# Softmax sums laid over 32 partitions of 48 numbers instead of 128 of 12, in a clustered attention and FFT-filter kernel

## The chip, the cores and the metric

One core of a Trainium2 chip runs the kernel. The metric is the device time of one execution in microseconds; the times of several executions are given by their median. The profile is of one execution. Its engines are PE (TensorE, matrix products), PEld (TensorE's weight loads), DVE (VectorE), ACT (ScalarE), POOL (GpSimd) and SP (SyncE, which here only issues transfers).

## The reference

Inputs are q, k, v of 4 batches x 8 heads x 768 tokens x 64 numbers, and 16 centroids for each head. Everything is float32.

```python
q_assign = np.argmax(np.einsum('bhsd,hcd->bhsc', q_n, c_n), axis=-1)     # q, k, c with unit norm
k_assign = np.argmax(np.einsum('bhsd,hcd->bhsc', k_n, c_n), axis=-1)
mask = q_assign[:, :, :, None] == k_assign[:, :, None, :]
scores = np.where(mask, scale * q @ k.T, -1e9)
attn = np.exp(scores - scores.max(-1)); attn = attn / (attn.sum(-1) + 1e-9)
x = (attn @ v)                                   # heads side by side: 4 x 768 x 512
x1, x2, x3 = split(x @ w_proj, 3)
y = x1 * irfft(rfft(x2) * rfft(filter)) * x3     # along the 768 tokens
out = y @ w_out
```

So each token attends to the tokens of its own cluster, and the result goes through a gated filter over the whole sequence (called the hyena in the code).

## The kernel before

The work is cut into eight groups n (a batch and half of its heads), each of two pairs pr of heads, and four hyenas, one for each batch, which follow when both groups of a batch are through.

For one pair, `attention` runs over six blocks sk of 128 keys. For each block TensorE makes the scores in three pieces of 512 columns (`sc`); the operands `aug` hold q or k in 64 rows and the cluster's one-hot rows (the mask) beside them, so that the mask comes out of the same product. ScalarE turns each piece into exponentials in `p` (`exp`, L647 and L650). TensorE multiplies them with v (`pv`, L661) into a pair of PSUM banks, and VectorE adds the blocks' exponentials up into `acc` (L682; the first two blocks are added in three pieces, L678, on VectorE or GpSimd).

`acc` then holds, for each of the 1536 queries of the pair, 128 partial sums, one on each partition. They are reduced in one of two ways. The first two groups and the last one (called `late` in the code) use a product with ones (`den`, L695). The ten other pairs use transfers: three GpSimd transfers add the upper half of the partitions onto the lower half (128 to 16 rows, L715); SP writes the 16 rows to DRAM (`dd`, L719) and reads them back spread over the partitions (`dp`, L721); VectorE sums the 16 rows (L725), adds a small constant (L726) and takes the reciprocal (L728). For every pair but the last, SP writes the reciprocals to DRAM (`dr`, L729) and reads them back to all partitions (`rb`, L732), and VectorE multiplies the attention's result with them into `xT` (L761), the hyena's input. The last pair's reciprocals are spread by products on TensorE.

The `routing` of group n + 1 runs beside the attention of group n: transposes of q and k (L551), products with the centroids (L583), comparisons on VectorE (L588 to L608) and transfers of the mask rows into `aug` (L482). The hyena multiplies xT with w_proj (L798), takes the spectrum, multiplies it with the filter's (L822, L826), transforms back, folds (L887, L897), gates (L862, L900) and multiplies with w_out.

Each step is recorded by `op` with the engines that may run it and a planned cost. The order of all 1936 steps, the engine of each and the PSUM banks are read from the string `ORDER`, written by a planner beforehand: `V694` is step 694 on VectorE, `P1421:0` step 1421 on TensorE in bank 0; A is ScalarE, G is GpSimd, S is SP. Each engine runs its steps in that order and waits at each for what the step needs. A step on GpSimd with `lock=True` also waits for the last VectorE step so marked, since both use one port.

At the start TensorE makes 16 warm-up products on the tile `y` (`hot`). The filter's values are loaded into the memory of `y` and `y2` (`tables`).

Of the kernel before, what the change touches and what calls it, by code (L numbers as in the profile page):

```python
# [27 lines left out]
EPS = 1e-30  # L28
# [101 lines left out]
P149:2 A99 P249:5 S128 G132 P251:4 A151 V93 V91 A250 V90 P243:7 A252 V92 S125 P183:6 V109 P245:5 A244 G98 V107 A184  # L130
S129 P185:0 P187:7 V150 G253 A186 P190:3 S288 V110 P192:6 P194:2 A188 V147 P200:0 V111 S287 A195 P202:7 V112 A246
P204:2 V199 A191 P189:45 V113 A193 V197 A201 A203 V198 P208:3 P210:6 A205 P212:0 V114 P216:7 P196 A211 V207 A209 A213
P218:2 P220:6 A254 P224:3 V148 P226:0 G154 V115 P206 A217 A219 V119 A118 P228:1 V153 P263:7 A116 V155 P214 V117 A221
V215 A248 P293:2 P222 A227 A294 V157 A229 P255:6 V223 A225 P257:0 P295:2 A264 P297:1 P300:3 A258 P261:7 A256 P302:0
V158 P230 A298 V160 A301 A262 V231 A296 P304:6 P310:1 S352 P312:3 A305 P267:72 S291 A303 V156 A232 S292 V159 A311
P233:6 S285 V269 A259 G162 P314:0 V268 S290 P318:1 A313 P299:45 V270 A315 G161 S289 A266 V234 P320:2 S286 P322:7 A319
V271 G152 P163:3 A323 S242 P171:0 A260 P164:6 S235 V272 P326:1 V273 G307 P328:7 A165 P306 A327 V166 A167 G358 P330:1
V274 A169 P316 G353 A331 V275 G309 A329 P334:3 P172:1 A321 V168 S278 P336:7 A175 G356 P177:2 V276 S280 V170 P324 A335
G308 S277 A173 V176 S279 V174 P419:361 S236 G247 A337 A181 V317 G357 A265 P338:0 P178:7 S453 A339 P332 S454 A421 V420
A422 V325 P359:0 A179 P361:1 P363:3 P340 A362 A360 V182 G426 A364 P366:6 V237 P368:1 A342 V180 P370:0 S238 G355 P376:3  # L140
P378:7 A371 V333 P365:45 S282 G354 A369 S455 A367 P380:2 A379 S283 P384:0 V374 P386:1 A381 P388:6 S281 P392:7 V341
A377 P372 S284 A387 S239 A385 P394:2 A389 S240 V375 P396:3 P343:1 A397 V373 A395 P427:063 V383 A393 A344 S345 P400:2
P402:7 A429 P404:1 V391 P382 A430 A428 A401 P461:0 A405 V399 P463:3 P465:6 A403 P390 A466 S346 A425 V407 P468:2
P435:17 S456 A464 V241 P470:6 P472:3 P398 A471 V437 A462 G476 V436 A473 P478:6 V438 P480:0 P482:1 P486:7 A481 P488:3
V347 P406 V439 A469 S348 A433 S458 V440 A483 P409:0 S418 V441 G475 A408 S459 P490:2 A489 P494:1 P467:45 V442 S460 A495
A487 S349 V443 G477 A410 P474 A479 A491 S446 V444 P496:3 S411 V485 P498:1 P502:7 A497 P701:062 S448 A434 S445 A424
V431 S447 P484 A499 V493 S350 S452 P504:3 P506:1 S457 P492 A505 V423 A704 S412 V501 A503 S520 P500 A507 S449 A703 S451
P639:3 V509 P508 A640 S738 A702 P641:7 V413 P643:1 A510 G708 P511:3 S414 A642 G432 P646:0 A644 V512 P648:2 P650:6 A647
G706 P656:7 S513 P658:1 A649 P660:3 P645:45 S450 V351 A657 A661 V653 A651 S416 P664:0 P666:2 A659 P668:7 V655 S415
P672:3 P674:6 A669 P676:1 V707 P652 A673 S514 V654 A677 A665 V663 P709:731 A675 A667 P680:0 V671 P682:6 S741 P684:2  # L150
A681 P662 A685 A711 V515 A683 V679 P743:0 S516 P670 A710 S740 A744 A712 S735 P745:2 V417 P747:6 P750:0 P752:1 P717:37
V687 A753 A746 S518 A748 S517 P754:1 A714 V718 P760:2 G689 P678 S736 V719 A755 G758 V720 S700 A751 P686 V721 P762:6
P764:3 A688 V722 P768:7 P770:1 P772:0 A761 V723 G757 P749:45 A765 A769 V724 P776:2 A771 P778:3 P780:7 P756 A779 V759
A763 V519 A705 G690 P766 V725 A781 V726 P521:1 S728 V767 S804 P523:3 A522 S729 A777 P531:6 S727 V525 A773 S732 V524
P526:7 A532 S730 V775 G691 P784:1 S739 P786:2 P528:0 A787 S742 A527 P533:3 A713 S734 V529 P788:6 P564:2 S733 V534 A789
S737 P774 V535 A785 G537 A715 V530 S692 A565 P805:7 V536 P807:6 P809:1 P812:3 A808 V539 P814:0 P816:2 A810 P782 V783
A806 A815 P822:6 A817 P824:1 P826:7 V538 A823 P830:0 P790 A813 V791 A831 A827 P540:2 S866 A792 P543:6 G819 V542 S693
P867:307 A825 V541 S731 V544 G821 P811:45 A869 V545 A870 V546 G793 A868 P548:1 V547 A873 P832:2 P834:6 V549 G716
P551:0 A833 P838:3 V550 P818 A835 G820 V552 A839 V553 P840:7 P842:2 V829 P875:163 A843 P556:0 V554 A877 S906 P828 A841
V837 A876 G794 A878 P846:2 P566:7 A847 V557 G555 P848:1 P850:3 V694 P909:6 P559:2 A910 P836 V695 V560 A851 S696 A871  # L160
V558 S903 G562 P911:6 V567 P568:3 S907 A912 V561 P913:0 P883:76 A569 G795 V845 S908 A879 S904 A849 P570:2 A914 S698
V884 G563 V885 P916:3 P918:1 P579:0 V886 A919 P920:6 P926:7 A580 P928:1 V887 A917 P844 A921 V853 A929 S796 P572:03
A927 P852 A573 V888 G855 V574 P930:6 G872 V575 P934:1 P581:7 A931 V889 A854 G576 S797 P936:0 P583:3 V582 A882 S901
P938:6 V890 P915:45 A584 A937 V891 G923 A939 P942:7 P922 A880 V571 S896 V577 A943 S894 V925 A874 P587:30 S697 V892
P585:6 V578 G856 S895 A588 A935 P932 S893 V586 G924 A881 S902 V589 V590 P944:2 S899 P946:7 V798 P950:1 P952:6 A947
S905 P594:0 V933 P596:3 A595 A951 P940 A953 V799 V941 S800 G857 A945 P954:7 S970 P1089:0 P598:1 A955 S898 A1090 V699
P1091:6 P1093:2 P1096:7 P1098:0 P948 V949 A1099 A1092 S801 A1097 P1100:0 S802 P1106:6 A1094 P956 V957 S858 A1107 A1101
P1108:7 P600:2 A958 V592 G959 P1110:6 V591 A1109 P1114:0 P1095:45 A599 G593 A1111 V601 V597 S859 P1116:7 P1118:1
P1151:623 A1117 G1105 A1115 A1119 P609:7 A1152 V1154 S1186 P602:01 A1153 V1103 S1187 P1159:236 V1104 A603 S897 A1158
V605 G1155 S900 V604 P1102 A1161 V1113 G960 S1191 A1162 S1190 A1160 P1122:0 P1124:1 A1123 P1167:23 S1192 V803 A610  # L170
G607 P1126:6 V1168 P1112 A1127 G606 V860 A1125 V1169 A1156 P1130:0 G961 P1132:7 V861 V1170 P1134:6 S862 A1131 P1193:1
P1195:2 P1197:3 P1120 A1196 V1121 A1135 A1198 P1200:0 A1133 P1202:2 V1171 P1204:6 P1210:3 A1194 P1212:7 P1128 A1203
S864 V1172 A1201 S1188 V1129 A1211 P611:1 S962 A1163 P1214:2 S863 P1218:0 A1166 P1220:3 V612 P1136 S1185 V1173 A1213
A1205 V1137 P1222:1 A1215 P613:7 A1138 P617:62 S963 A1221 P1199:45 V608 A618 S1189 A614 V1174 P1226:3 P1228:7 P1206
A1227 V620 G1208 A1223 V1175 A1219 P1230:3 V619 A1229 P1216 G1139 S1178 V1176 A1231 G622 S1177 A1157 V964 P1234:1
S1183 P615:0 A1164 V965 G621 P1224 S966 V616 S1180 V1207 S1179 P1236:2 V1209 P1232 A1237 V865 A1235 A1165 P1238:6 V623
P1325:730 S967 A1239 V1217 S968 G1140 P1317:216 S1150 A1328 S1182 A1326 V1225 A1327 S1254 P1240 A1320 S1184 A1319
S1181 A1318 P1255:0 V1233 P1257:3 P1259:7 A1256 P626:1 A1260 A1258 P624:2 P1262:6 V969 G1141 P631:0 A625 A627 V1241
P1264:7 P629:3 A1265 A1263 P981:2 V630 G1243 P971:1 V1321 P973:7 G1324 A972 S1142 A982 P983:6 G1323 V975 A1242 S628
V974 P976:3 A632 V984 P978:1 A977 V985 P1266:2 P1272:7 V979 P1014:0 A1267 S1143 V980 P1274:3 P1276:6 S1352 V987  # L180
P1280:2 A1275 P1261:45 G1244 A1273 V986 S1358 A1281 V988 A1015 S1356 P1282:1 P1284:3 V989 P990:7 A1283 S1351 P1288:2
G1269 P993:0 V991 A1289 P1016:1 S1355 V992 A1285 P1018:2 V994 A1277 G1270 S1316 P1020:7 V1017 A1019 V995 P998:3 G996
# [46 lines left out]
def build(T):  # L229
# [386 lines left out]
    def attention(n, pr, sins):  # L616
# [88 lines left out]
        if not last:  # L705
# [5 lines left out]
            else:  # L711
# [12 lines left out]
                def gather(e):  # L724
                    T.nc.vector.tensor_reduce(T.dn, T.dp[:].rearrange("p r b -> p b r"), axis=AX, op=Alu.add)  # L725
                    T.nc.vector.tensor_scalar(T.dn, T.dn, EPS * S, None, op0=Alu.add)  # L726
# [467 lines left out]
```

## Time and profile before

| what | value |
|---|---|
| median of 3 runs | 366.29 us (366.25 to 366.62) |
| the profiled execution | 366.52 us |
| its span on the core | 364.7 us |
| PE busy | 353.9 us (97%) |
| DVE busy | 339.3 us (93%) |
| ACT busy | 271.1 us (74%) |
| POOL busy | 137.1 us (38%) |
| granted TensorE clock, mean | 0.996 |

Busy is the time in which the engine ran at least one instruction; the span goes from the first instruction to the last, and the difference to the execution's own time lies around it. "L661" is line 661 of the kernel before. A row of a group gives the line, the engine, the operation, the tiles written and read, their shapes, the count, and behind the bar the busy time in us and the mean of one in ns, then the time that the engine idled before them and what ended it. In a timeline row the start and the length come first, and idle time before it stands in brackets with what ended it.

### The profile page before, as it was taken

Reading aid. Unit: us, or ns where it says so; the run is one execution under the profiler, and the core shown is the slowest. Engines: PE = TensorE matmul, PEld = TensorE weight load, DVE = VectorE, ACT = ScalarE, POOL = GpSimd, SP = SyncE. Lnnn points to the kernel's source line nnn. Section 1 sums busy time; section 2 is a strip of 40 time slices with the busy share of each in tenths; the row PEclk is TensorE's granted clock in tenths of the full one; section 3 lists DMA queues with packets and bytes.
Section 4 is the critical chain, followed back from the end, with each engine's and each line's share of the span. In section 5 each row is a group of like instructions: output and inputs, shape, how many; then the busy total and the mean of one; then the engine's idle time right before and its main releaser. Section 6 shows DMA issues by size and latency. Waiting matters only on the chain.

```text
span 364.7 us, 8483 instructions
## 1 busy us (share of the span) xinstructions
PE 353.9 (97%) x3254; PEld 198.8 (55%) x3254; DVE 339.3 (93%) x470; ACT 271.1 (74%) x502; POOL 137.1 (38%) x167
## 2 busy tenths in 40 slices
PE   8799999999999999999999999999999999999994
PEld 4445445454555555665565555555655556475771
DVE  8899889998999999989987999999999999999992
ACT  5999989789878777898987667789969826532232
POOL 8930841122131644344143463432340363045500
PEclk9999999999999999999999999999999999999998
DMA  9990999165576568678667948375755640410214
GB/s 171 226 248 14 218 180 179 26 166 132 120 134 147 102 108 129 130 148 151 131 125 193 174 111 155 43 156 56 178 80 155 89 61 17 162 43 2 117 59 173
DMA packets 88004, 45.69 MB, mean 125 GB/s; under 512 B 76488, under 2 KB 82012, under 8 KB 87964
## 3 DMA queue, kind: packets, MB, share of 16 engines
q1 hardware_dynamic: 84076, 35.16, 40.9%
q0 software_dynamic: 2960, 9.77, 18.6%
q8 instruction: 25, 0.41, 0.5%
q10 hardware_dynamic: 928, 0.23, 0.3%
q14 instruction: 15, 0.12, 0.1%
HBM read 31.59 MB, written 7.40 MB: 107 GB/s over the span
## 4 chain that ended last, share of the span: by engine, by line
PE 77%; DVE 9%; ACT 8%; DMA 3%; issue 2%; SPq 0%; DVEq 0%
PE bank L69 33%; PE pair L661 26%; PE bank L798 6%; PE bank L551 4%; ACT p L650 3%; DVE acc L682 3%; PE bank L583 2%; DMA dn<-dd 2%; PE bank L1015 2%; ACT aug L246 2%; ACT p L647 2%; PE bank L67 2%; DMA aug<-ohT 1%; PE bank L695 1%; PE bank L470 1%
## 5 line engine op out<-in xcount | busy, mean ns | idle before, releaser
L661 PE MATMUL pair<-p,vraw 128*64 128x385 f32 x768 | 140.4, 488 | 0.0
L650 ACT ACTIVATE p<-bank 128x512 f32<-128x512 f32 x192 | 108.5, 614 | 18.0 <-PE bank L69 15.6
L682 DVE TENSOR_TENSOR acc<-p,acc 128x1536 f32<-128x1536 f32 x64 | 112.1, 1751 | 2.1
L661 PEld LDWEIGHTS pair<-p,vraw 128*64 128x64 f32 x768 | 54.5, 136 | 47.6 <-issue 38.8
L69 PE MATMUL bank<-aug,aug 80*64 80x256 bf16 (+3 forms) x708 | 78.9, 327 | 1.3 <-DMA aug<-ohT 0.7
L647 ACT ACTIVATE p<-bank 128x512 f32<-128x512 f32 x96 | 57.8, 613 | 16.8 <-PE bank L69 11.3
L69 PEld LDWEIGHTS <-aug 80*64 80x64 bf16 (+1 forms) x708 | 40.9, 109 | 42.4 <-issue 29.7
L715 POOL DMA_DIRECT2D acc<-acc x30 | 24.1, 805 | 75.1 <-DMA acc<-acc 30.6
L678 POOL TENSOR_TENSOR acc<-p,p 128x512 f32<-128x512 f32 x23 | 29.8, 1298 | 48.6 <-ACT p L650 13.6
L69 PE MATMUL bank<-xT,wpj 128*64 128x384 bf16 x480 | 46.3, 326 | 0.0
L69 PEld LDWEIGHTS <-wpj 128*64 128x64 bf16 x480 | 27.6, 110 | 15.8 <-issue 5.3
L246 ACT CAST aug<-qkP 64x768 bf16<-64x768 f32 x43 | 35.4, 829 | 0.7
L246 ACT COPY qkP<-bank 128x512 f32<-128x512 f32 (+1 forms) x56 | 28.4, 562 | 7.9 <-PE bank L69 5.8
L69 PEld LDWEIGHTS <-y 128*64 128x64 bf16 x480 | 23.8, 110 | 11.5 <-issue 2.4
L822 DVE TENSOR_TENSOR tm<-bank,hm 128x512 f32<-128x512 f32 x44 | 27.9, 682 | 0.9 <-POOL y L826 0.2
L826 POOL TENSOR_TENSOR y<-tm 128x512 bf16<-128x512 f32 x17 | 21.5, 1275 | 13.9 <-DVE tm L822 8.7
L69 PE MATMUL bank<-wout,y 128*64 128x512 bf16 x192 | 23.1, 379 | 0.0
L798 PE MATMUL bank<-wpj,xT 128*64 128x512 bf16 x192 | 21.9, 379 | 0.0
L248 POOL CAST aug<-qkP 64x768 bf16<-64x768 f32 x17 | 13.9, 827 | 20.5 <-DVE dn L728 8.3
L246 ACT COPY ob<-bank 128x512 f32<-128x512 f32 x21 | 12.2, 594 | 11.0 <-PE bank L69 9.3
L900 POOL TENSOR_TENSOR y<-yy,x 128x768 bf16<-128x768 f32 x7 | 13.1, 1868 | 18.7 <-DVE yy L897 13.8
L551 PE MATMUL bank<-ident,qkraw 128*128 128x128 f32 x144 | 18.1, 276 | 0.0
(161 smaller groups left out, 447.2 us busy)
## 6 DMA issues: line engine op xcount, KB each, us to landing
qkraw<-in_k_dram SPq DMA_DIRECT2D x32, 192.0 KB
vraw<-in_v_dram SPq DMA_DIRECT2D x16, 384.0 KB
qkraw<-in_q_dram SPq DMA_DIRECT2D x31, 192.0 KB
rb<-dr SPq DMA_DIRECT2D x30, 192.0 KB
out_dram<-ob SPq DMA_DIRECT2D x11, 512.0 KB
acc<-acc POOLq DMA_DIRECT2D x10, 384.0 KB, 5.0
acc<-acc POOLq DMA_DIRECT2D x10, 192.0 KB, 3.9
wpj<-in_moe_w_proj_dram POOLq DMA_DIRECT2D x4, 384.0 KB, 6.3
```

Of the source, the lines that this page charges most:

```text
L69: T.nc.tensor.matmul(out[64 * i:64 * i + 64], lhsT[:, 64 * i:64 * i + 64], rhs, start=start, stop=stop)
L246: T.nc.scalar.copy(out, in_)
L551: T.nc.tensor.transpose(bank(h.ids[i // 4])[:, block(i % 4, 2 < i < NT)], raw(ss[i // NT], i % NT), T.ident)
L647: T.nc.scalar.activation(o, ap(h).rearrange("p (a b) -> p a b", a=2), Act.Exp, scale=0.125)
L650: T.nc.scalar.activation(flat(s)[:, lo:lo + 512], ap(h), Act.Exp, scale=0.125)
L661: T.nc.tensor.matmul(o[64 * hp:64 * hp + 64, ch, :385], T.vraw[vs][:, hp, sk * D:(sk + 1) * D], T.p[slots[sk]][:, hp, 384 * ch:384 * ch + ...
L678: alu(e).tensor_tensor(o, x, y, op=Alu.add)
L682: T.nc.vector.tensor_tensor(T.acc[os], T.p[slots[sk]][:, :, :S], T.acc[os], op=Alu.add)
L715: op(("POOL", .8), lambda e, rows=rows: T.nc.gpsimd.dma_start(flat_()[:rows], flat_()[rows:2 * rows], accum_op=Alu.add), te, r=[], w=AK, b ...
L798: T.nc.tensor.matmul(ap(h)[64 * i:64 * i + 64], T.xT[xs][:, kt, tokens(m, i, w_)], T.wpj[:, kt, DM:2 * DM], start=kt == 0, stop=kt == ND - 1)
L822: op(("DVE", .68), lambda e, i=i, cs=cs, r=r, h=h: T.nc.vector.tensor_tensor(T.tm[r][:, cs], ap(h), hmrow(i, (0, 2, 2, 3)[2 * r + cs]), op ...
L826: op({"POOL": 1.3, "DVE": .68}, lambda e, i=i, r=r: alu(e).tensor_tensor(T.y[:, i, r], T.tm[r][:, 0], T.tm[r][:, 1], op=Alu.add if r else ...
```

## The change

The tile `dp` becomes 32 partitions of 16 x 48 numbers, where it was 128 of 16 x 12, and a tile `dn2` of 32 x 48 takes the sums; the write to `dr` follows. The sum (`gather`) may now run on GpSimd also, by halving additions. The filter loads are recorded as waiting for the warm-up products. The string `ORDER` is replaced as a whole: banks, places and the engines of some 50 steps differ. `gather` stands on GpSimd once among its ten steps (`G1594`), otherwise on VectorE. Lines behind 383 move by up to nine.

```diff
 ORDER = """
-A35 V0 G18 S45 A46 P14:0 G29 S47 V22 P6:1 G20 S48 P5:2 G28 P11:3 S52 P1:4 G23 P2:5 V36 V53 S51 P16:6 G34 V37 P13:7 V59
...
+A35 V0 G18 S48 A45 P8:0 G20 S47 V22 A46 G25 P11:1 G27 S50 P15:2 A49 P12:3 G29 S52 A51 P14:4 G23 P7:5 V36 V53 P13:6 V37
...
                     T.f[w_][64 * e_:64 * e_ + 64, 0:1 if e_ else 3:2], fv(w_)[:, e_:e_ + (1 if e_ else 3):2]), 16.0,
-                   w=[("f", w_, e_)], byts=131e3 * (2 - e_), kind="load", after=got)
+                   r=[("hot", i) for i in range(HOT)], w=[("f", w_, e_)], byts=131e3 * (2 - e_), kind="load", after=got)
...
-                op(("SP", .6), lambda e: T.nc.sync.dma_start(T.dp, T.dd[os].rearrange("r (p b) -> p r b", b=12)),
-                   te + 4, r=[("dd", os)], w=["dp"], byts=236e3, lat=1.0)
+                op(("SP", .6), lambda e: T.nc.sync.dma_start(T.dp, T.dd[os].rearrange("r (p b) -> p r b", b=48)),
+                   te + 4, r=[("dd", os)], w=["dp"], byts=237e3, lat=1.0)
 
                 def gather(e):
-                    T.nc.vector.tensor_reduce(T.dn, T.dp[:].rearrange("p r b -> p b r"), axis=AX, op=Alu.add)
-                    T.nc.vector.tensor_scalar(T.dn, T.dn, EPS * S, None, op0=Alu.add)
-                op(("DVE", .68), gather, te + 6, r=["dp"], w=["dn"], kind="port")
-            op(("DVE", .23), lambda e: T.nc.vector.reciprocal(T.dn, T.dn), te + 6, r=[], w=["dn"])
-            op(("SP", .6), lambda e: T.nc.sync.dma_start(T.dr[os].rearrange("z (a b) -> (z a) b", b=12), T.dn),
+                    if e == "POOL":
+                        rows, w = ROWS, T.dp[:].rearrange("p r b -> p (r b)")
+                        while rows > 1:
+                            rows //= 2
+                            T.nc.gpsimd.tensor_tensor(w[:, :rows * 48], w[:, :rows * 48], w[:, rows * 48:2 * rows * 48], op=Alu.add)
+                        T.nc.gpsimd.tensor_scalar(T.dn2, w[:, :48], EPS * S, None, op0=Alu.add)
+                        return
+                    T.nc.vector.tensor_reduce(T.dn2, T.dp[:].rearrange("p r b -> p b r"), axis=AX, op=Alu.add)
+                    T.nc.vector.tensor_scalar(T.dn2, T.dn2, EPS * S, None, op0=Alu.add)
+                op({"DVE": 1.3, "POOL": 2.9}, gather, te + 6, r=[], w=["dn", "dp"], lock=True)
+            dn_ = lambda: T.dn if late else T.dn2
+            op(("DVE", .23), lambda e: T.nc.vector.reciprocal(dn_(), dn_()), te + 6, r=[], w=["dn"])
+            op(("SP", .6), lambda e: T.nc.sync.dma_start(T.dr[os].rearrange("z (a b) -> (z a) b", b=12 if late else 48), dn_()),
                te + 7, r=["dn"], w=[("dr", os)], byts=6e3)
...
-               r=["hot"], w=[h], alloc=h, free=[h])
+               r=["hot"], w=[h, ("hot", i)], alloc=h, free=[h])
...
-    T.dn, T.rb, T.dp = tl([128, 12], F32, "dn"), tl([128, S], F32, "rb"), tl([128, ROWS, 12], F32, "dp")
+    T.dn, T.rb, T.dp = tl([128, 12], F32, "dn"), tl([128, S], F32, "rb"), tl([32, ROWS, 48], F32, "dp")
+    T.dn2 = tl([32, 48], F32, "dn2")
```

More of the change, by code (lines that the diff above doesn't have):

```diff
@@ L130 @@
[L130 to L149, printed above, removed]
@@ L226 @@
+S1927
 """
```

181 lines of the change are left out of this document (100 added, 81 removed).

## The prediction, made before the changed kernel ran

> **What bounds the kernel now.** I read the page first, then busy time by stage, the groups of instructions by shape, the waits, and the timelines of VectorE and TensorE around the places where one hands over to the other. The page:
>
> ```profile
> span 364.7 us, 8483 instructions
> PE 353.9 (97%) x3254; PEld 198.8 (55%) x3254; DVE 339.3 (93%) x470; ACT 271.1 (74%) x502; POOL 137.1 (38%) x167
> PE 77%; DVE 9%; ACT 8%; DMA 3%; issue 2%; SPq 0%; DVEq 0%
> ```
>
> TensorE is busy 97% of the span and makes 77% of the chain that ended last. The change leaves its work alone (the same products; the built programs differ by two matmuls of 2762), so the end can move only by what TensorE waits for. VectorE is the second engine, at 93%. By stage (columns: PE, PEld, DVE, ACT, POOL busy):
>
> ```profile
> 20.00:80.00 60.00, 58.91 (x456) 29.32 (x456) 56.61 (x68) 55.51 (x102) 19.17 (x26) 1.00 0.70 146
> 80.00:160.00 80.00, 80.00 (x722) 43.28 (x720) 77.36 (x94) 66.85 (x123) 26.65 (x27) 1.00 0.63 127
> 160.00:200.00 40.00, 39.91 (x358) 23.53 (x356) 35.48 (x45) 33.00 (x61) 15.99 (x17) 1.00 0.75 149
> 200.00:280.00 80.00, 79.35 (x745) 45.35 (x743) 77.30 (x102) 62.95 (x118) 30.33 (x28) 1.00 0.64 122
> 280.00:340.00 60.00, 60.00 (x605) 34.81 (x603) 58.61 (x90) 29.87 (x59) 24.72 (x20) 1.00 0.30 64
> ```
>
> From 80 to 340 us TensorE idles 0.74 us in all; the granted clock is 1.00. VectorE idles 260 - 248.75 = 11.25 us there, nearly half of it in 160:200. So VectorE is no bound yet, but its room is small, and the change works on VectorE. How close the two run shows where the third batch's filter stage (the hyena) begins:
>
> ```profile
> 279.58 1.01 DVE L761 SCALAR_TENSOR_TENSOR xT<-osb,rb 128x768 bf16<-128x768 f32 x1
> 281.04 0.61 PE L69 MATMUL bank<-aug,aug 80*64 80x256 bf16 x6
> 281.48 1.89 PE L798 MATMUL bank<-wpj,xT 128*64 128x512 bf16 x16
> ```
>
> The last quarter of xT ends at 279.58 + 1.01 = 280.59 us, and the product that reads it starts at 281.48: 0.9 us of margin.
>
> **Sum of exponentials on VectorE.** The groups by shape (mean ns after the comma, idle before behind the second bar):
>
> ```profile
> L725 DVE TENSOR_REDUCE dn<-dp 128x12 f32<-128x192 f32 x10 | 4.8, 482 | 0.0
> L726 DVE TENSOR_SCALAR dn<-dn 128x12 f32<-128x12 f32 x10 | 3.4, 339 | 0.3
> L728 DVE RECIPROCAL dn<-dn 128x12 f32<-128x12 f32 x15 | 3.3, 218 | 0.7 <-DMA dn<-dd 0.6
> L596 DVE TENSOR_REDUCE mx<-sim 128x48 f32<-128x768 f32 x7 | 6.7, 951 | 0.2
> L509 DVE TENSOR_REDUCE mx<-sim 128x24 f32<-128x384 f32 x2 | 1.1, 552 | 0.1
> L678 POOL TENSOR_TENSOR acc<-p,p 128x512 f32<-128x512 f32 x23 | 29.8, 1298 | 48.6 <-ACT p L650 13.6 <-DVE oh L603 11.6 <-DVE acc L682 11.6
> ```
>
> A reduce's time goes by the elements of one partition. L596 and L509, which read neighbours, give (951 - 552) / 384 = 1.04 ns for each and 152 ns to start. By that L725 with 192 would take 352 ns; it took 482, 130 more, and it reads with a step (48 B now, 192 B after). After the change each of 32 partitions holds 16 x 48 = 768 elements. If the 130 ns is fixed, the reduce takes 951 + 130 = 1.08 us; if it goes by elements, 951 + 4 x 130 = 1.47 us. The added constant takes 339 + 36 x 1.04 = 0.38 us, so one sum takes 1.46 to 1.85 us where 0.82 is taken now. The nearest row, L725 itself, speaks for the upper end, L596 with the same 768 elements for the lower; I take the middle, 1.65, 0.83 more each. The Trainium skill, SBUF — State Buffer, section "Door 1: The DMA port swizzle", says that accesses which leave a 16-byte line each time pay a penalty; by that rule the extra goes by elements, a sum takes 1.85 us, and the stall below grows by 8 x 0.2 = 1.6 us. The 130 ns of L725 agree with a penalty, but no run here shows how it grows. Against the whole idea stands the Trainium skill, Trainium Kernel Development and Optimization, "Best Practices" (always tile to 128 partitions).
>
> In the built order nine of the ten sums stay on VectorE and one (the ninth, near 290 us) goes to GpSimd. There it is four additions with 720 results in all plus a scalar; at L678's 1298 / 512 = 2.5 ns that is 1.8 us and up to 2.9 with five starts. It gives VectorE back 0.82 us.
>
> **Transfers.** Each dp transfer falls from 2048 pieces of 48 B to 512 of 192 B, in all 15,360 of these packets:
>
> ```profile
> q1 hardware_dynamic: 84076, 35.16, 40.9%
> SPq L729 <- DVE dn L728: 37.7, 11, 9.1
> ```
>
> I price this at nothing: L725 idles 0.0 us before its ten executions, so no sum waits for dp. What does wait is SP's queue, 37.7 us in eleven waits, for the reciprocal; a later sum holds up the loads and mask writes queued behind dr. I let the loads' buffers cover that.
>
> **The new order.** It changes the engine of some 50 steps. Ahead of the xT step at 279.58 VectorE gets four more part sums (L678), two y products (L900), two folds (L897) and three qkP copies, and loses three aug casts, four short copies and L703:
>
> ```profile
> L678 DVE TENSOR_TENSOR acc<-p,p 128x512 f32<-128x512 f32 x25 | 17.3, 717 | 0.2 <-ACT p L650 0.2
> L900 DVE TENSOR_TENSOR y<-yy,x 128x768 bf16<-128x768 f32 x5 | 4.8, 951 | 0.0
> L897 DVE TENSOR_TENSOR yy<-sd 128x384 f32<-128x384 f32 x15 | 7.9, 537 | 1.1 <-POOL y L900 0.8
> L248 DVE COPY qkP<-bank 128x512 f32<-128x512 f32 x2 | 1.4, 686 | 1.5 <-PE bank L551 1.5
> L248 DVE COPY qkP<-bank 128x384 f32<-128x384 f32 x2 | 1.1, 552 | 0.1
> L248 DVE CAST aug<-qkP 64x768 bf16<-64x768 f32 x4 | 2.2, 551 | 0.0
> L248 DVE COPY inv<-bank 64x192 bf16<-64x192 bf16 x3 | 0.7, 236 | 0.0
> ```
>
> That is 4 x 0.72 + 2 x 0.95 + 2 x 0.54 + 2 x 0.69 + 0.55 = 7.8 added, and 3 x 0.55 + 4 x 0.24 + 0.56 = 3.2 taken away. With some 0.3 for starts that overlap, VectorE has 4.3 us more. Eight sums ahead of this place add 8 x 0.83 = 6.6 (5.1 to 8.2), eight wider reciprocals 8 x 36 x 1.04 ns = 0.3. In all 11.2 us (9.7 to 12.8) more before the xT step. Ahead of the first hyena's xT the same count gives no net change, so all of it falls between 107 and 280 us. TensorE has three more score pieces ahead of its product, some 0.5 us by the row at 281.04.
>
> What can cover it are the waits of VectorE:
>
> ```profile
> 43.34 0.75 DVE L446 SCALAR_TENSOR_TENSOR hm<-bank,hw,tm 128x512 bf16<-128x512 f32 x1 [0.87 <-POOL acc L678]
> 48.52 1.41 DVE L446 SCALAR_TENSOR_TENSOR hm<-bank,hw,tm 128x512 bf16<-128x512 f32 x2 [0.69 <-ACT tm L442]
> 55.09 0.23 DVE L728 RECIPROCAL dn<-dn 128x12 f32<-128x12 f32 x1 [0.56 <-DMA dn<-dd]
> 86.01 0.56 DVE L703 TENSOR_SCALAR den<-bank 128x384 f32<-128x384 f32 x1 [1.13 <-ACT p L647]
> ...
> 162.38 0.69 DVE L248 COPY qkP<-bank 128x512 f32<-128x512 f32 x1 [1.53 <-PE bank L551]
> 184.92 0.56 DVE L862 TENSOR_TENSOR x<-bank,x 128x384 f32<-128x384 f32 x1 [0.79 <-PE bank L69]
> 196.72 0.69 DVE L248 COPY ob<-bank 128x512 f32<-128x512 f32 x1 [0.32 <-PE bank L69]
> 199.31 1.28 DVE L810 TENSOR_TENSOR uv<-tm,bank 128x512 bf16<-128x512 f32 x2 [1.42 <-PE bank L798]
> 243.49 1.02 DVE L862 TENSOR_TENSOR x<-bank,x 128x384 f32<-128x384 f32 x2 [0.17 <-ACT x L246]
> 246.93 0.56 DVE L897 TENSOR_TENSOR yy<-sd 128x384 f32<-128x384 f32 x1 [0.80 <-POOL y L900]
> ```
>
> Those behind 107 us sum to 5.0. In them VectorE was ahead of another engine; work put before them is free. With the 0.9 of margin and TensorE's 0.5 the cover is 6.4, and 11.2 - 6.4 = 4.8 us of TensorE's waiting would be left. The four early waits (3.25 us) are cover only if the new order starts later work sooner. I count the first three, 2.1 us, since the order of the filter's spectra and the first denominators is rewritten, and not the fourth, behind the exponentials: 2.7 us left. TensorE waits for this in the mask writes before it or at the hyena itself; the delays of one queue are counted once.
>
> **The first stage.** The first score product waited here:
>
> ```profile
> 18.35 0.38 PE L67 MATMUL bank<-aug,aug 80*128 80x512 bf16 x1 [0.79 <-DVE aug L248]
> ```
>
> The new order writes first the two mask rows that it reads, so up to 0.79 us goes; but ScalarE's exponentials still queue behind its copies, and I take 0.3. Three loads go from SP's queue to ScalarE's, at a time when ScalarE has no input yet. The filter loads named as waiting for the warm-up products did so already, for they overwrite the tile that these read.
>
> **The sum.** The profiled execution took 366.52 us: a span of 364.7 and 1.8 around it. 366.5 + 2.7 - 0.3 = 368.9; the median of the runs is 0.23 below the profiled one, so the forecast is 368.7 us.
>
> **Rivals.** *Faster:* the reduce costs 1.08 us (sum 1.46), all waits of the table fill (8.3 us), and 9.7 - 8.3 - 0.9 - 0.5 leaves nothing. The first score's 0.3 comes in, and the one late wait of TensorE as well if the mask chain gets shorter:
>
> ```profile
> 239.49 0.84 PE L69 MATMUL bank<-aug,aug 80*64 80x512 bf16 x8 [0.65 <-DMA aug<-ohT]
> ```
>
> That gives 366.3 - 0.95 = 365.3 us. It decides for this if VectorE's added work before 280 us stays under 9.7 us. For it speaks that the steps were set anew with GpSimd at 38%; against it that only one sum went there, while GpSimd gave up work to the others. *No change:* what is left of the stall and the 0.3 cancel, 366.3. *Slower by more:* the sum at 1.85 and no early cover, 12.8 - 6.4 = 6.4: 372.7 less the 0.3, 372.4 us; the place is the mask chain at 239.49 or the product at 281.48. The idea that the sums mostly move to GpSimd and unload VectorE is out, as the built order shows one of ten there.
>
> **Chances.** About 0.2% (0.7 us) is what a measurement of this kernel can tell from no change. Forecast 0.45, slower by more 0.19, no change 0.12, faster 0.24. The range 365.3 to 372.0 leaves out the last part of the slower case and little of the faster one. Slower 0.64, same 0.12, faster 0.24.
>
> **What would show it.** In the changed profile: the reduce at 1.1 to 1.5 us; VectorE busy 346 to 350 us; its waits between 107 and 280 mostly gone; TensorE waiting for mask writes or for xT, 2 to 3 us in sum between 200 and 330 us; the first score near 18 us. The forecast is wrong if TensorE's busy share from 80 to 340 us stays at all but 1 us, or if the reduce takes under 1.1 us.

## The result and the profile after

The changed kernel takes 370.52 us (median of 5, 369.24 to 371.19) where the kernel before takes 366.42 us in the same session (366.25 to 366.65): a ratio of 1.0104, 95% interval 1.0087 to 1.0121. In a later session it took 369.70 us against 366.46, ratio 1.0088 (1.0074 to 1.0102). It is slower by 3.2 to 4.1 us. The forecast was 368.7, a loss of 2.3 us, with the range 365.3 to 372.0. The first and third line of the page and its chain of work that ended last:

```profile
span 368.7 us, 8481 instructions
PE 356.1 (97%) x3256; PEld 207.3 (56%) x3256; DVE 347.6 (94%) x468; ACT 274.8 (75%) x511; POOL 132.4 (36%) x163
PE 65%; DVE 15%; ACT 11%; issue 4%; DMA 2%; ACTq 1%; POOL 1%; DVEq 0%; POOLq 0%
```

VectorE is busy for 8.3 us more. Its share of the chain went from 9 to 15%, ScalarE's from 8 to 11%, and TensorE's fell from 77 to 65%. The view by stage (PE, PEld, DVE, ACT, POOL busy):

```profile
20.00:80.00 60.00, 59.45 (x460) 28.49 (x459) 55.97 (x64) 56.66 (x107) 21.32 (x32) 0.97 0.63 142
80.00:160.00 80.00, 80.00 (x716) 45.96 (x718) 78.12 (x94) 68.72 (x125) 24.23 (x24) 1.00 0.68 132
160.00:200.00 40.00, 39.35 (x345) 22.79 (x343) 38.51 (x48) 32.53 (x59) 12.10 (x14) 1.00 0.67 127
200.00:280.00 80.00, 78.26 (x734) 47.27 (x730) 78.70 (x103) 60.78 (x114) 28.20 (x27) 1.00 0.61 128
280.00:340.00 60.00, 59.09 (x581) 35.65 (x579) 58.67 (x84) 32.51 (x63) 24.29 (x21) 1.00 0.27 69
```

Between 80 and 340 us VectorE now idles 260 - 254.00 = 6.0 us instead of 11.25, and TensorE 260 - 256.70 = 3.30 us instead of 0.74. TensorE loses nothing between 80 and 160 us; the loss lies in the three last stages. These waits have grown by 2.56 us and the span by 4.0. TensorE's busy time has grown as well, from 353.9 to 356.1 us with two products more, and no run here takes apart why. The groups of the changed steps by shape, and the sum on GpSimd from its timeline:

```profile
L732 DVE TENSOR_REDUCE dn<-dp 32x48 f32<-32x768 f32 x9 | 13.3, 1478 | 0.0
L733 DVE TENSOR_SCALAR dn<-dn 32x48 f32<-32x48 f32 x9 | 1.6, 175 | 0.3
L736 DVE RECIPROCAL dn<-dn 32x48 f32<-32x48 f32 x10 | 4.4, 435 | 0.1
L736 DVE RECIPROCAL dn<-dn 128x12 f32<-128x12 f32 x5 | 1.1, 213 | 0.0
287.53 2.46 POOL L729 TENSOR_TENSOR dp<-dp 32x384 f32<-32x384 f32 x4 [3.11 <-DVE acc L682]
290.08 1.85 POOL L730 TENSOR_SCALAR dn<-dp 32x48 f32<-32x48 f32 x1
```

The reduce takes 1478 ns where it took 482. The reciprocal of 48 columns takes 435 ns, that of 12 still 213. The one sum on GpSimd begins at 287.5 us and ends at 291.9. And these are TensorE's longest waits in its timeline between 100 and 340 us (idle time and what ended it in brackets):

```profile
162.95 0.82 PE L67 MATMUL bank<-inv,y 128*128 128x192 bf16 x8 [0.46 <-DVE x L870]
208.03 0.84 PE L69 MATMUL bank<-xT,wpj 128*64 128x384 bf16 x8 [0.63 <-ACT ob L246]
228.38 0.84 PE L69 MATMUL bank<-xT,wpj 128*64 128x384 bf16 x8 [0.30 <-ACT p L647]
277.45 1.05 PE L69 MATMUL bank<-wout,y 128*64 128x512 bf16 x8 [0.28 <-ACT p L650]
279.14 1.05 PE L69 MATMUL bank<-wout,y 128*64 128x512 bf16 x8 [0.41 <-ACT p L650]
321.08 0.85 PE L695 MATMUL bank<-acc,ones 128*32 128x384 f32 x8 [0.49 <-DVE acc L682]
324.33 0.55 PE L751 MATMUL bank<-ident,den 128*128 128x128 f32 x3 [0.31 <-ACT x L246]
```

Seven small waits, 2.88 of the 3.30 us. None of them is ended by a mask write or by xT: the two products with xT, at 208.03 and 228.38, wait for ScalarE. Most name ScalarE, but ScalarE was itself held up, as its timeline tells:

```profile
207.39 0.58 ACT L246 COPY ob<-bank 128x512 f32<-128x512 f32 x1 [0.87 <-DMA out_dram<-ob]
276.81 0.60 ACT L650 ACTIVATE p<-bank 128x512 f32<-128x512 f32 x1 [1.31 <-DVE acc L682]
323.80 0.86 ACT L246 COPY x<-bank 128x384 f32<-128x384 f32 x2 [1.25 <-DVE y L908]
```

At 276.81 the exponential waits 1.31 us until VectorE has added an older block, because only then is a buffer `p` free; while it waits, ScalarE empties no PSUM bank, and TensorE waits until 277.45. In VectorE's timeline of the microseconds before, the sum stands in the way:

```profile
271.28 1.45 DVE L732 TENSOR_REDUCE dn<-dp 32x48 f32<-32x768 f32 x1
272.77 0.18 DVE L733 TENSOR_SCALAR dn<-dn 32x48 f32<-32x48 f32 x1
272.87 1.01 DVE L905 TENSOR_TENSOR yy<-sd 128x384 f32<-128x384 f32 x2
273.81 0.43 DVE L736 RECIPROCAL dn<-dn 32x48 f32<-32x48 f32 x1
274.17 0.88 DVE L908 TENSOR_TENSOR y<-yy,x 128x768 bf16<-128x768 f32 x1
274.98 1.73 DVE L682 TENSOR_TENSOR acc<-p,acc 128x1536 f32<-128x1536 f32 x1
```

The starts follow one another without a gap; the addition at 274.98 ends at 276.71 and is the one that frees the buffer. The wait at 208.03 is of another kind: ScalarE waited there for a write of the output (more below).

### The profile page after: what moved, and what is told of

It is laid out like the page before. It is cut to its first block, busy times and chain, and to the rows that moved or that the text cites. A ratio compares the mean times of both kernels' runs of the same rounds, so it can differ in the third digit from the quotient of the medians.

```text
span 368.7 us, 8481 instructions
## 1 busy us (share of the span) xinstructions
PE 356.1 (97%) x3256; PEld 207.3 (56%) x3256; DVE 347.6 (94%) x468; ACT 274.8 (75%) x511; POOL 132.4 (36%) x163
## 2 busy tenths in 40 slices
DMA packets 71684, 45.69 MB, mean 124 GB/s; under 512 B 60168, under 2 KB 65692, under 8 KB 71644
## 4 chain that ended last, share of the span: by engine, by line
PE 65%; DVE 15%; ACT 11%; issue 4%; DMA 2%; ACTq 1%; POOL 1%; DVEq 0%; POOLq 0%
PE bank L69 26%; PE pair L661 25%; PE bank L806 4%; DVE acc L682 4%; PE bank L551 3%; ACT p L650 2%; PE bank L583 2%; DMA out_dram<-ob 2%; ACT p L647 2%; PE bank L67 2%; ACT aug L246 2%; ACT qkP L246 1%; DVE tm L830 1%; DVE dn L732 1%; ACT osb L685 1%
## 5 line engine op out<-in xcount | busy, mean ns | idle before, releaser
L661 PE MATMUL pair<-p,vraw 128*64 128x385 f32 x768 | 142.0, 492 | 0.2 <-ACT osb L685 0.2
L650 ACT ACTIVATE p<-bank 128x512 f32<-128x512 f32 x192 | 109.8, 613 | 21.8 <-PE bank L69 17.8
L682 DVE TENSOR_TENSOR acc<-p,acc 128x1536 f32<-128x1536 f32 x64 | 112.0, 1750 | 2.1
L69 PE MATMUL bank<-aug,aug 128*64 128x512 bf16 (+3 forms) x708 | 78.9, 326 | 0.3
L647 ACT ACTIVATE p<-bank 128x512 f32<-128x512 f32 x96 | 58.2, 616 | 10.2 <-PE bank L69 8.8
L69 PEld LDWEIGHTS <-aug 128*64 128x64 bf16 (+1 forms) x708 | 42.6, 109 | 37.9 <-issue 26.9
L69 PE MATMUL bank<-xT,wpj 128*64 128x384 bf16 x488 | 48.5, 326 | 0.9 <-ACT ob L246 0.6
L246 ACT CAST aug<-qkP 64x768 bf16<-64x768 f32 x50 | 41.3, 830 | 0.9
L69 PEld LDWEIGHTS <-wpj 128*64 128x64 bf16 x488 | 31.7, 109 | 14.0 <-issue 6.3
L69 PEld LDWEIGHTS <-y 128*64 128x64 bf16 x480 | 25.3, 110 | 11.2 <-issue 3.5
L248 POOL CAST aug<-qkP 64x768 bf16<-64x768 f32 x13 | 10.9, 842 | 30.5 <-DVE acc L682 22.7
L246 ACT COPY x<-bank 128x384 f32<-128x384 f32 x24 | 11.6, 488 | 11.2 <-PE bank L69 5.8
L551 PEld LDWEIGHTS bank<-ident,qkraw 128*128 128x128 f32 x144 | 15.6, 141 | 4.7 <-issue 2.1
```

The lines of the kernel that those rows point to most:

```text
L69: T.nc.tensor.matmul(out[64 * i:64 * i + 64], lhsT[:, 64 * i:64 * i + 64], rhs, start=start, stop=stop)
L246: T.nc.scalar.copy(out, in_)
L551: T.nc.tensor.transpose(bank(h.ids[i // 4])[:, block(i % 4, 2 < i < NT)], raw(ss[i // NT], i % NT), T.ident)
L647: T.nc.scalar.activation(o, ap(h).rearrange("p (a b) -> p a b", a=2), Act.Exp, scale=0.125)
L650: T.nc.scalar.activation(flat(s)[:, lo:lo + 512], ap(h), Act.Exp, scale=0.125)
L661: T.nc.tensor.matmul(o[64 * hp:64 * hp + 64, ch, :385], T.vraw[vs][:, hp, sk * D:(sk + 1) * D], T.p[slots[sk]][:, hp, 384 * ch:384 * ch + ...
```

## The experiments

Theory A: VectorE's time decides. The wider sum and reciprocal fill its queue, and what follows in it comes late. Rivals: the new order is the cause, or the longer way of each chain of factors from its sum to the multiplications. In the expectations A is this theory throughout; what the other letters stand for each of them says itself. Ratios are to runs of the kernel before on the same chip.

**Shape alone, in the old order.** The edit is that of the change without the new `ORDER`; all ten sums stay on VectorE.

> The order and engines of the kernel before, with the 32 x 48 shape; all ten sums on VectorE. Theory A (VectorE's longer sums eat its room, and TensorE pays): by the changed kernel's rows each sum takes 1.478 + 0.175 where 0.482 + 0.339 stood, and its reciprocal 0.435 where 0.218 stood, 10 x 1.05 = 10.5 us more VectorE work; with 5.0 us of waits behind 107 us and 0.9 of margin to fill, 2.5 to 5 us slower than before: 369 to 371.5. Theory B (the new order and its engines do it, the shape costs nothing): within 0.7 us of 366.4. Theory C (shorter transfers help, the order spoils it): under 365.7.

Measured 373.45 us, ratio 1.0205 (1.0191 to 1.0219), a loss of 7.2 us. The shape costs more than the whole change, and more than the 371.5 us that theory A gave it at most. The reduce takes 1476 ns. The line of the page:

```profile
PE 357.5 (96%) x3254; PEld 206.5 (56%) x3254; DVE 349.3 (94%) x470; ACT 271.7 (73%) x502; POOL 137.3 (37%) x167
```

**Order alone, with the old shape.** The edit is the new `ORDER` in the kernel before, with `G1594` written as `V1594`, since the old sum runs on VectorE only.

> The new order and engines with the old 128 x 12 shape; all ten sums on VectorE. Theory A: VectorE has only the 4.3 us of moved steps more than before, under the 6.4 us that can cover them: 365.7 to 367.1, no change to be told. Theory B: it keeps the loss, 369.5 to 371. Theory C: slower than before by over 2 us as well.

Measured 365.83 us, ratio 0.9997 (0.9982 to 1.0012): no difference. The order by itself is not the cause. The constant, L726, takes 174 ns here. The line of its page and its stages from 80 to 340 us:

```profile
PE 355.3 (97%) x3256; PEld 209.2 (57%) x3256; DVE 338.5 (93%) x470; ACT 274.6 (75%) x511; POOL 128.3 (35%) x158
```
```profile
80.00:160.00 80.00, 80.00 (x717) 45.96 (x717) 77.13 (x95) 68.72 (x124) 24.62 (x25) 1.00 0.69 133
160.00:200.00 40.00, 39.81 (x351) 23.14 (x349) 36.33 (x47) 32.65 (x60) 11.75 (x14) 1.00 0.73 129
200.00:280.00 80.00, 79.61 (x751) 48.88 (x747) 76.74 (x104) 63.16 (x118) 28.14 (x27) 1.00 0.62 130
280.00:340.00 60.00, 60.00 (x597) 38.09 (x593) 58.38 (x91) 30.52 (x58) 22.68 (x18) 1.00 0.29 64
```

With the same places for all other work, TensorE idles 0.58 us in these stages and 3.30 us with the new shape. Against this kernel the change's span is 3.6 us longer, 368.7 against 365.1, and 2.7 us of that are these waits. TensorE's busy time by itself is no measure of the loss: 355.3 us here, at the same time as 353.9 before.

**The reduce made cheaper by reading neighbours.** In the changed kernel the sum reads 16 neighbours instead of 16 numbers 192 B apart, so it adds up the wrong numbers:

```diff
-T.nc.vector.tensor_reduce(T.dn2, T.dp[:].rearrange("p r b -> p b r"), axis=AX, op=Alu.add)
+T.nc.vector.tensor_reduce(T.dn2, T.dp[:].rearrange("p r b -> p (r b)").rearrange("p (b r) -> p b r", r=ROWS), ...)
```

> The changed kernel with one thing changed: the reduce on VectorE reads the 768 numbers of a partition as neighbours instead of with a step of 192 B (so it adds up the wrong numbers; same transfers, same count). Both theories expect the reduce at 0.95 us where it took 1.48 if the step is what it pays for, 1.48 if not. Theory A: nine times 0.53 = 4.8 us less VectorE work gives back half of the loss or more, 367 to 368.5 us. Theory B: no change, 370.5.

Measured 367.42 us, ratio 1.0029 (1.0017 to 1.0040). Of the loss of 3.2 to 4.1 us some 2.2 to 2.8 come back with the step of 192 B alone (0.0059 to 0.0075 of the ratio):

```profile
PE 356.7 (98%) x3256; PEld 207.9 (57%) x3256; DVE 343.3 (94%) x468; ACT 274.6 (75%) x511; POOL 132.3 (36%) x163
```
```profile
L732 DVE TENSOR_REDUCE dn<-dp 32x48 f32<-32x768 f32 x9 | 8.4, 932 | 0.0
```

**All ten sums on GpSimd.** In `ORDER` the letter of the nine other sums becomes G.

> The changed kernel with all ten sums on GpSimd at the same places of the order. Theory A: VectorE loses nine times 1.65 = 14.9 us of work and gets the room of before back; if GpSimd's own queue does not hold the sums up (one took 4.3 us there), 365 to 367.5 us. Theory B: no gain, 370.5 or more. A third outcome, over 371: the sums queue on GpSimd behind its transfers and reach xT too late.

Measured 381.10 us, ratio 1.0419 (1.0402 to 1.0436). VectorE is busy for 337.3 us, less than before, and yet this is by far the slowest kernel: the sums come late, and VectorE's queue behind them with them. The wait stands in one group:

```profile
L736 DVE RECIPROCAL dn<-dn 32x48 f32<-32x48 f32 x10 | 4.4, 440 | 21.3 <-POOL dn L730 21.3
```

VectorE reaches each reciprocal before GpSimd has its sum and waits, up to 3.5 us at a time and 21.3 us in all, with the following work queued behind. Busy and waiting together are 358.6 us.

**The same work behind the reciprocal.** In the order-alone kernel, nine of the ten chains get work into an unread tile `jk` (128 x 12):

```diff
...
+            def inv_(e, extra=not late and COUNT_() % 10 < 9):
+                T.nc.vector.reciprocal(T.dn, T.dn)
+                if extra:
+                    for _ in range(2):
+                        T.nc.vector.tensor_reduce(T.jk, T.dp[:].rearrange("p r b -> p b r"), axis=AX, op=Alu.add)
+                    T.nc.vector.reciprocal(T.jk, T.jk)
+            op(("DVE", .23), inv_, te + 6, r=[], w=["dn"])
...
```

`COUNT_` counts the chains.

> The new order with the old shape (365.83 us when run before), and on VectorE, behind the reciprocal of nine of the ten chains, two further sums of 0.49 us and a reciprocal of 0.22 us into a tile that nobody reads: 1.19 us per chain, about what the new shape adds, but behind the reciprocal, so that the factors set off no later. Theory A (the loss is VectorE's time: whatever stands in its queue delays what follows): VectorE busy 338.5 + 9 x 1.19 = 349 us, and the time by the slope between the kernel with neighbours (343.3 busy, 367.42) and the changed one (347.6, 370.52), 0.72 us per us, 371.5, range 369.5 to 373. Theory B (the loss is the longer way of each chain of factors from its sum to the multiplications that wait for it): no loss, 365.5 to 366.5.

Measured 369.41 us, ratio 1.0079 (1.0065 to 1.0093). That the factors do not wait for the added work shows in the timelines of VectorE and of SP's queue, here at the first of the nine chains:

```profile
131.83 0.22 DVE L737 RECIPROCAL dn<-dn 128x12 f32<-128x12 f32 x1
131.97 0.96 DVE L740 TENSOR_REDUCE jk<-dp 128x12 f32<-128x192 f32 x2
132.08 0.34 SPq L743 DMA_DIRECT2D dr<-dn  x1
```

The write of the factors starts 0.03 us behind the end of their reciprocal, while the added sums run on to 132.93; in eight of the nine chains it starts within 0.05 us. (The view of the waits names an added sum as what released these writes; by the times it was the reciprocal.) Each chain is as long as in the order-alone kernel from its sum to its write, and still 3.0 us are lost against it by the ratios, 3.6 by the medians: the loss does not need a longer chain. It also comes with the old transfers. ScalarE's exponentials wait 2.1 us for the additions of L682 (L690 in this kernel), as in the change (2.0) and not as in the order alone (0.7). The added work was smaller than expected, 338.5 to 346.8 us:

```profile
PE 356.2 (97%) x3255; PEld 206.6 (56%) x3256; DVE 346.8 (94%) x497; ACT 274.9 (75%) x511; POOL 128.2 (35%) x158
```

So 369.41 lies just under the range of theory A, which was worked out for 349 us; by the line between the kernels with 345.8 and 347.6 us in the table below, 346.8 gives a ratio of 1.0080 (1.0072 with the change's ratio of the later session).

**The reciprocal over 12 columns.** In the changed kernel `reciprocal(dn_()[:, :12], dn_()[:, :12])`; 36 of the 48 columns are left as sums.

> The changed kernel with the reciprocal of the ten small sums over the first 12 of the 48 columns alone (the other 36 columns are left as sums, so three quarters of the factors are wrong numbers). The reciprocal falls from 0.435 to about 0.22 us, VectorE's busy time by 2.1 us to 345.5. Theory A: 0.72 us per us, 370.5 - 1.5 = 369.0 us, range 368.3 to 369.7. Theory B (only the length of the chain): 0.2 us on each chain is nothing beside the sum's 1.0 us, 370.0 to 370.6.

Measured 368.47 us, ratio 1.0051 (1.0033 to 1.0069), as theory A had it. The reciprocal alone costs some 1.4 to 1.9 of the 3.2 to 4.1 us (0.0037 to 0.0053 of the ratio):

```profile
PE 356.1 (97%) x3255; PEld 207.8 (57%) x3256; DVE 345.8 (94%) x468; ACT 274.6 (75%) x511; POOL 132.4 (36%) x163
```
```profile
L736 DVE RECIPROCAL dn<-dn 32x12 f32<-32x12 f32 x10 | 2.1, 210 | 0.1
```

**No reduce at all.** The order-alone kernel with `tensor_scalar(T.dn, T.dp[:, 0, :], 100.0, ...)` in place of the reduce and the constant: the sum is left out.

> The new order with the old shape, and the sum over 16 rows left out: the constant (a larger one) is added to the first row alone, so the factors are wrong numbers. VectorE loses ten sums of 0.49 us, 338.5 to 333.6 us busy, and each chain becomes 0.49 us shorter. Theory A with the cover that the trace shows (TensorE is idle for 0.58 us between 80 and 340 us in the new order with the old shape, so nothing is left to be had): 365.3 to 366.0 us, no gain. Rival (the time follows VectorE's busy time below the old amount too, at half a us per us): 363.0 to 364.0 us.

Measured 365.86 us, ratio 0.9981 (0.9972 to 0.9991). VectorE falls by 4.5 us and the median stays where the order alone had it, 365.86 against 365.83. By the ratios it is 0.6 us less, and the intervals overlap. A cheaper sum than the old one has at most that to win here.

```profile
PE 354.2 (97%) x3255; PEld 208.0 (57%) x3256; DVE 334.0 (92%) x460; ACT 274.4 (75%) x511; POOL 128.2 (35%) x158
```

**Ten sums on VectorE.** The changed kernel with `G1594` put back to `V1594`.

> The changed kernel with the one sum that is on GpSimd put back to VectorE at the same place of the order, near 287 us: VectorE gets 1.48 + 0.18 = 1.65 us more, and the chain loses GpSimd's four additions and constant of some 4.3 us. Theory A: VectorE's time decides, 349.3 us busy, 370.5 + 0.72 x 1.65 = 371.7 us, range 370.9 to 372.3. Rival (the slow sum on GpSimd holds up the hyena behind it by as much as it relieves VectorE): 369.8 to 370.7 us.

Measured 371.91 us, ratio 1.0146 (1.0131 to 1.0161). The one sum on GpSimd saves some 1.5 to 2.1 us (0.0042 to 0.0058 of the ratio). Without it TensorE gets a wait that the changed kernel does not have:

```profile
289.93 1.05 PE L806 MATMUL bank<-wpj,xT 128*64 128x512 bf16 x8 [0.94 <-DVE uv L818]
```
```profile
PE 356.0 (96%) x3255; PEld 207.3 (56%) x3256; DVE 349.1 (94%) x470; ACT 274.9 (74%) x511; POOL 128.2 (35%) x158
```

This is the moved sum itself: it stands at 287.05 us on VectorE, and the product L818 behind it, which empties TensorE's banks, comes late. Another wait, 1.10 us for a mask row (aug<-ohT) at 256.79, stands 30 us ahead of the only step that differs, so the moved sum can't have made it; the second profile of the change has 0.20 us at that product. The page, beside that of the shape alone (349.3 us, ratio 1.0205), tells what the new order is worth with the new shape: 0.6%, some 2 us, at the same busy time.

All kernels in the new order by VectorE's busy time:

| kernel | DVE busy, us | ratio |
|---|---|---|
| no reduce | 334.0 | 0.9981 |
| order alone | 338.5 | 0.9997 |
| neighbours | 343.3 | 1.0029 |
| reciprocal over 12 | 345.8 | 1.0051 |
| work behind the reciprocal | 346.8 | 1.0079 |
| the change | 347.6 | 1.0104 |
| ten sums on VectorE | 349.1 | 1.0146 |

This speaks for theory A: in one order, two shapes, three kinds of added work and two places in the chain lie on one curve. Its first 4.5 us cost nothing clear of the noise, the next 4.8 (338.5 to 343.3) cost 1.2 us, the last 5.8 cost 4.3 (0.0117 x 366.4). With the change's ratio of the later session, 1.0088, the order of the rows stays. The curve holds for this order alone: the shape in the old order lies 2 us above it at the same busy time. All ten on GpSimd fits it, if the waits are counted as busy time, a reading made after the result: at 358.6 us, 9.5 beyond the last row, it takes 9.2 us more.

**Three runs on the start.** The changed kernel's profile has the granted clock at half from 21.3 to 24.7 us, in the view by microsecond (the last three columns are the clock, the DMA share and GB/s; the last row holds the three microseconds before):

```profile
21.00:22.00 1.00, 0.89 (x5) 0.29 (x3) 0.58 (x1) 1.00 (x3) 0.00 (x0) 0.65 1.29 256
23.00:24.00 1.00, 1.00 (x6) 0.46 (x4) 1.00 (x3) 1.00 (x4) 0.00 (x0) 0.50 1.06 232
24.00:25.00 1.00, 1.00 (x6) 0.30 (x6) 1.00 (x3) 0.98 (x3) 0.00 (x0) 0.64 1.17 254
18.00:21.00 3.00, 1.94 (x10) 0.78 (x10) 2.80 (x7) 2.96 (x7) 2.38 (x9) 1.00 1.16 226
```

I ran the changed kernel again, and it and the order alone with five unread transposes of the unit matrix in TensorE's waits:

```diff
+EXTRA = {187: 3, 192: 2}
...
+        for _ in range(EXTRA.get(o.seq, 0)):
+            nc.tensor.transpose(T.bank[5][:, :128], T.ident, T.ident)
         o.fn(o.on)
```

> The changed kernel as it is, for more executions. In its profile the granted clock of TensorE falls to 0.50 for some 3.4 us from 21.3 us, after TensorE was busy for only 0.57 to 0.71 of each us from 18 to 21; the profiles of the old order do not show it, those of the new order show it sometimes. Of the five executions so far, those with a mean granted clock of 0.992 to 0.995 took 370.52, 370.52 and 371.19 us, those with 1.000 took 369.24 and 370.19. Theory C (part of the loss is this fall of the clock): again two groups, 369.2 to 370.2 us at 0.997 and above, 370.5 to 371.2 us below. Rival (the start has room, the fall costs nothing at the end): no relation between clock and time, all within 369.2 to 371.2.

> The changed kernel with five transposes of the unit matrix on TensorE, into a bank that is free then and that nobody reads: three ahead of the third score of the first block (where TensorE waited 0.43 us) and two ahead of the fifth (0.29 us), some 0.14 us each. Theory C: the granted clock stays at 1.00 between 21 and 25 us in the profile, no execution has a mean under 0.996, and the median falls to that of the undisturbed group, 369.3 to 370.0 us. Rival (no cost at the end): 370.2 to 370.8 us, or more by what the added products hold up (0.7 us at most).

> The new order with the old shape, and the same five transposes: the one candidate among these kernels for a time under that of before. Its executions without the transposes took 365.58 to 366.44 us at a mean clock of 0.997 and above (eight), 366.93 to 368.04 below (three). Theory C: all at 365.6 to 366.0, ratio to before 0.998 to 0.9995. Rival (the fall of the clock has another cause than TensorE's waits at 18 to 21 us, or the transposes hold up the scores): some executions at 367 to 368 as before, median 365.8 to 366.4.

Measured: the change again 369.70 us (369.18 to 370.07), with transposes 369.74 (369.11 to 369.97), the order alone with transposes 365.98 (365.60 to 367.75), ratio 0.9986 (0.9971 to 1.0001). In the profile with the transposes the clock stays up; the same view of the changed kernel:

```profile
18.00:21.00 3.00, 2.62 (x14) 1.31 (x15) 2.59 (x6) 2.98 (x6) 2.18 (x8) 1.00 1.17 237
21.00:25.00 4.00, 3.78 (x30) 1.87 (x30) 3.79 (x7) 3.98 (x9) 0.00 (x0) 1.00 1.23 251
```

By itself that says little, since the clock also stays at 1.00 there in four profiles of this order without them. The sixteen executions with transposes say more: each has a mean clock of 0.997 or above, where it is 0.992 to 0.995 in seven of the twenty-one without.

The medians do not move: 369.74 against 369.70, both in the range of theory C. Whether the fall costs time stays open. Of the ten executions of the change without transposes, four have a mean clock of 0.992 to 0.995 and take 370.07 to 371.19 us, 370.6 in the mean; the six others take 369.18 to 370.19, 369.7 in the mean; the five with transposes take 369.11 to 369.97. In the order alone it is 367.6 us for three executions and 365.9 for eight. Such a difference, 0.9 us in the change, is what theory C expects, but the low execution of the second session (370.07 us) lies among the others. Three of five were low in the first session and one of five in the second, which would account for the better part of the 0.9 us between the losses of 4.1 and 3.2 us.

No version with the right result beats the kernel before beyond the measurement (the one without the reduce does, by 0.7 us). The interval of the order alone with transposes reaches 1.0001, and three of its eleven executions took 367.29 to 367.75 us at a mean clock of 0.998 and above, against theory C's 366.0 at most. The profiled one of them (367.75 us) shows most of it, in TensorE's and ScalarE's timelines (lines stand one further down there):

```profile
207.25 0.84 PE L70 MATMUL bank<-xT,wpj 128*64 128x384 bf16 x8 [1.21 <-ACT ob L247]
```
```profile
206.61 0.58 ACT L247 COPY ob<-bank 128x512 f32<-128x512 f32 x1 [1.45 <-DMA out_dram<-ob]
```

A write of the output is late in some executions, ScalarE waits for its buffer and TensorE for ScalarE. It is the 0.63 us at 208.03 in the profile of the change, too; in the second profile of the same kernel it is absent (370.07 us). That part of the 3.30 us is chance and not the change.

## Why the prediction was right, and where its steps were off

**The bound and the mechanism held.** TensorE's end moves by what it waits for, VectorE's room is small, the change fills it, and what the room does not hold comes out as waits of TensorE behind 160 us. VectorE's busy time, 347.6 us, lies in the 346 to 350 forecast; TensorE idles 2.65 us between 200 and 340 us where 2 to 3 were forecast up to 330, 0.63 of it by the late output write. VectorE's waits between 107 and 280 us went from 5.0 us to four of 1.7 us in all, the longest of them:

```profile
199.49 1.29 DVE L818 TENSOR_TENSOR uv<-tm,bank 128x512 bf16<-128x512 f32 x2 [0.91 <-PE bank L806]
```

**The size came out near by errors that cancel, and that part is luck.** The prediction put 11.2 us more of VectorE's work ahead of the last xT step of the third hyena, against 8.5 us of cover. In the traces that step starts at 279.58 us before, at 281.74 with the order alone and at 284.76 after the change; VectorE is busy for 263.36, 264.10 and 272.38 us up to there. So 9.0 us were added: 0.7 by the order, where 4.3 were taken, and 8.3 by the shape, where 6.9 were. VectorE's idle time ahead of the step shrank by 3.8 us, from 16.2 to 12.4, where waits of 5.0 + 2.1 were counted as cover, and all of that lies behind 107 us: the 2.1 of early cover did not come. The step stands 5.2 us later, and TensorE's first product of the hyena 3.5 us later (285.02 against 281.48), where 2.7 were forecast. So the added work was taken 2.2 us too high, and the cover, 5.5 us in all (9.0 - 3.5), by 3.0.

**One sum: the total was exact, by two errors that cancel.** The reduce sits at the upper end, 1.478 us, and the constant at 0.175 instead of 0.38: 1.65 together, the value taken. The 130 ns do go by elements: 527 ns more for 768 (1478 against the 951 of L596), 0.69 ns each, where 130 for 192 are 0.68. That is the step that the prediction left open between "fixed" and "by elements". By the Trainium skill's rule on 16-byte lines, which the prediction cited from SBUF — State Buffer, "Door 1: The DMA port swizzle", this end was the right one; the trace agrees, 1478 ns with a step and 932 among neighbours. The constant had been priced from a mean of 339 ns that held executions from 173 to 637; in the new order with the old shape it takes 174.

**The reciprocal was the term that was mis-sized.** I priced 36 further columns at 1.04 ns each, 0.04 us, as for a sum. It takes 0.222 us more (435 ns against 213 in the same profile), 6.2 ns per column: 1.8 us for the eight ahead of the xT step where 0.3 were taken, 2.2 for all ten. Given back alone it returns 1.4 to 1.9 us of time (368.47). The Trainium skill, VectorE: DVE Perf Modes, section "First, the fixed hardware budget", describes the reciprocal as an iterative divide with a repeat count of 8. It gives no price for it; the rows here give six times that of a sum's element.

**The place was wrong.** Not the mask writes and not xT: the 0.65 us wait for the mask before is gone (the second profile of the change has 0.20 us for a mask, at 256.51), and TensorE does not wait at the third hyena's first product. The lateness goes another way: VectorE frees the buffers of the exponentials and the banks late, ScalarE waits for them, and TensorE for ScalarE. This path is read from the traces; what was tested is the work on VectorE. With ten sums on VectorE the third hyena has a wait, at 289.93, but for VectorE to empty a bank and not for xT. Nor does the cover end sharply: the curve charges a quarter of each us at first and near all of it later.

**Transfers and queues.** Priced at nothing; packets fell from 88,004 to 71,684, and both shapes lie on the one curve. SP's waits for the reciprocal grew from 37.7 us (eleven) to 56.2 (fifteen), 47.2 of it with the order alone, and TensorE's waits for masks stayed at 0 to 0.20 us.

**The sum on GpSimd** was priced at 1.8 to 2.9 us and took 4.3, its last instruction alone 1.85 for 48 numbers; it was still worth having, 1.5 to 2.1 us. With all ten sums there that instruction takes 0.32 to 0.35 us in nine of them, in which VectorE mostly stood waiting for it, and 1.77 in the ninth, the same sum as in the change. What VectorE does beside it, in the change first and then with all ten on GpSimd:

```profile
289.98 1.75 DVE L682 TENSOR_TENSOR acc<-p,acc 128x1536 f32<-128x1536 f32 x1
298.28 1.75 DVE L682 TENSOR_TENSOR acc<-p,acc 128x1536 f32<-128x1536 f32 x1
298.44 1.77 POOL L730 TENSOR_SCALAR dn<-dp 32x48 f32<-32x48 f32 x1
```

In both the constant lasts until 0.2 us behind the end of VectorE's large addition. That GpSimd has to wait the addition out fits all eleven executions; no run was made to test it.

**The order and the start.** Of the order's 4.3 us on VectorE ahead of the third hyena 0.7 came, and they were no loss by themselves (order alone: 0.9997); VectorE's busy time as a whole fell by 0.8 us. By the two strings 62 steps change their engine, not some 50. The start: the first score piece came 0.17 us earlier, at 18.18 us. TensorE is busy 75.54 us up to 80 us, 75.31 before, but 3.4 us of that are at half the clock, so no run shows the 0.3 by itself.

**Rivals.** "Faster" was to be decided by added work under 9.7 us before 280 us. Counted up to the xT step that came true, 9.0, and the kernel is slower all the same, because the waits did not fill as counted: the sign was badly chosen. The cheap reduce, its other condition, did not come. "Slower by more" had the reduce right and no early cover, also right; its 372.4 us lie 1.9 above the measured time, since the constant was cheap (1.6 us for eight) and the order added less.

## What to carry to other kernels

Price a re-laid tile per instruction by the elements of one partition, with the row of the same access (a step is not neighbours) and the same operation (a reciprocal's element is not a sum's): fewer partitions multiply all of it. Here an engine at 93% busy that only feeds the bound had room of a few us at a quarter of the price, and then each us on it cost nearly one, ahead of the reciprocal as behind it. Such room is not the sum of the engine's waits: 7.1 us were counted and 3.8 filled. Moving work to a slower idle engine helps only where the result isn't asked for at once: one sum of ten saved 1.5 to 2.1 us, ten cost 10.6 against the change.

## What the runs showed of the hardware

A strided reduce of float32 numbers pays 0.69 ns per element on top of 1.04 (1478 ns for 768 with a step of 192 B, 932 to 951 among neighbours), and 0.68 at a step of 48 B (482 ns for 192, against 352 worked out). A reciprocal costs 6.2 ns per element of a partition between 12 and 48 elements (213 and 435 ns), on 32 partitions as on 128 (210 and 213 ns for 12).

A GpSimd instruction of 0.32 to 0.35 us took 1.77 and 1.85 us beside an addition of 1.75 us on VectorE.

TensorE's granted clock fell to 0.50 for 3.4 us in the profile of the change although TensorE had been busy for 1.94 of the 3.00 us before and had idled 0.43 us at most at a time. The same 1.94 of 3.00 left it at 1.00 in the run with all sums on GpSimd; with 2.62 of 3.00 it stayed at 1.00 too. The Trainium skill, TensorE: Matmul & The Clock Gate, "Part 1: The HAM clock gate", has a free-running window of about 3.4 us and the same kernel varying with its phase, which agrees with the length and with a fall in some executions only; it names an idle window as the condition, and here two thirds of busy time did not prevent the fall.
